# One set of angle products for both last-stage tables, sine scales from columns, and short fillers, in a fused Fourier and channel-mix kernel

## The chip, the cores and the metric

The kernel runs on one core of one Trainium2 chip. The metric is the device time of one launch in microseconds (us), the median of several runs. A core has a matrix engine (PE in the profile, with its weight loads as PEld), a vector engine (DVE), a scalar engine (ACT), a gather and iota engine that also issues the loads (POOL) and an issuing engine for stores (SP). Each works through its own instructions in the order of the program.

## The reference

```python
X = np.fft.fft(x, axis=1)          # x: 8 x 3072 x 256
X = np.fft.fft(X, axis=2)
x = X.real
x_prev = np.concatenate([zeros, x[:, :-1, :]], axis=1)
xk = mu_k * x + (1.0 - mu_k) * x_prev
xr = mu_r * x + (1.0 - mu_r) * x_prev
k = np.maximum(xk @ w_k, 0.0)      # 256 -> 1024
v = k * k @ w_v                    # 1024 -> 256
r = 1.0 / (1.0 + np.exp(-(xr @ w_r)))
out = r * v
```

## The kernel before, in words

The real part of the two-dimensional transform is built from small dense products with tables of sines that the kernel makes itself. For each of 8 batches, `fold` (L144) adds each row of x to its mirrored row on DVE, in two halves of 9 and 8 rows a partition. Stage A (`a_sum` L475 in batch 0, `a_item` L457 later) multiplies the folded rows by the table `w_pm`. Stage D (`d_units` L497) multiplies by the table `w_eo` and leaves `g_all`. The last stage (`c_item` L529) multiplies `g_all` by the table `m_cs`, which has two planes (cosine and sine, index c) of 28 slices (two for each of the NJ = 14 columns j). `halves`, `diff`, `mix_part` and `mix` then make the shifted and mixed inputs on DVE, and 48 chunks of 512 tokens go through `k_products` (L614), a ReLU on ACT (L632), a square on DVE (L639), `v_tile` (L653), `r_item` with a sigmoid (L641) and `v_out` (L664).

The last part of the program is a loop over 197 steps that is full of matmuls; the code up to L750 is the start of batch 0, written out by hand. `pin_order` (L90) fixes the order on each engine to the order in which the code is written. This is the part that the change touches.

Tables. Each table is a sine of an angle. The angles are made as outer products: rows of 128 numbers on one partition (`rw`, L267, filled by DVE with `memset` and `ts`, L255) are multiplied on PE by another such row (`outer`, L293). DVE converts the product from PSUM to whole numbers (`ts` with a factor), wraps it with a bitwise and, and ACT takes the sine.
- `w_pm`: four products with rows P0, P1, E0, E1 (L300), the conversion `u_w` (L354, L355), two sines and a scaling (L356 to L359).
- `m_cs`: `m_outer(j0, j1)` (L337) makes for both c three products (Q2, RR, PH + c; a fourth, D0 + c, for j = 0). `m_angles` and `m_wrap` (L346, L350) convert, `m_sine` (L405) takes the sine. They are called for j 0 to 4 at the start, 5 to 8 while x is loaded, 9 to 13 after stage D (L706 to L708, sine at L750).
- `w_eo`: two products (L366), conversion `ueo` (L371), sine at L432, two columns copied from PSUM (L439).
- `turn`: a permutation table, rows at L379 (called at L700), columns by PE at L388 (step 2 of the loop), `turn_table` (step 3).
- The mixing factors are turned into columns by four one-column matmuls (`mu_turn`, L205), copied at L703.

PSUM is used through two rings of slots: three of 1024 columns (`ps_w`) and two of 512 (`ps_v`). A new user of a slot waits until the last one has been read.

`keep_busy` (L182) issues fillers, matmuls of zeros with 512 columns: 8 at the very start, 7 before stage A (L687), 4 before the first `k_products` (L743).

Loads of x go out on POOL in the order of L225 to L235, with iotas for their row indices between them; the weights follow in `loads` (L415).

Of the kernel before, what the change touches and what calls it, by code (L numbers as in the profile page):

```python
# [9 lines left out]
FP32 = mybir.dt.float32  # L10
# [29 lines left out]
def kernel(  # L40
# [10 lines left out]
    nc = tc.nc  # L51
# [7 lines left out]
    NJ, NJ1, NJ2 = 14, 5, 9  # L59
# [22 lines left out]
    def ps_v():  # L82
        return ps_slot("V", 2, 512)
# [98 lines left out]
    def keep_busy(n, ps=None):  # L182

        ps = ps or ps_v()
        for _ in range(n):
            nc.tensor.matmul(out=ps[:, 0:512], lhsT=zeros, rhs=_v(zeros, 0, [(0, 4), (1, P)]),  # L186
                             start=True, stop=True)

    keep_busy(8)


    mu_row = const.tile([1, 2, 256], FP32)
    mu_p = const.tile([1, 2, 2, P], FP32)
    unit = const.tile([1, 1], FP32)
    V.memset(unit, 1.0)
    for i, mu in enumerate((moe_mu_k, moe_mu_r)):
        nc.sync.dma_start(out=mu_row[:, i], in_=mu.rearrange("(a b) -> a b", a=1))

    def mu_rows(a):
        for p0, f0, step, n in (((0, 0, 1, 1), (1, 2, 2, 63), (64, 1, 2, 64)),  # L200
                                ((0, 128, 1, 1), (1, 254, -2, 63), (64, 255, -2, 64)))[a]:
            nc.scalar.activation(out=mu_p[:, a, :, p0:p0 + n],
                                 in_=_v(mu_row, f0, [(256, 2), (step, n)]), func=AF.Copy)

    def mu_turn():  # L205
        ps = ps_w()
        for a in range(2):
            for i in range(2):
                nc.tensor.matmul(out=ps[:, 2 * a + i:2 * a + i + 1], lhsT=mu_p[:, a, i], rhs=unit,
                                 start=True, stop=True)  # L210
        return ps
# [3 lines left out]
    for xm in xm_sb:  # L215
# [8 lines left out]

    iota(ramp, pattern=[[1, P]], base=0, channel_multiplier=0)  # L225
    load_p(0, 0)
# [10 lines left out]
    m_pi = const.tile([P, 1], FP32)  # L237
    V.memset(m_pi, -math.pi)
    p_pi = const.tile([P, 1], FP32)
    V.memset(p_pi, math.pi)  # L240


# [9 lines left out]
    nc.scalar.activation(out=m_cs.rearrange("p c s t -> p (c s t)").bitcast(FP32),  # L252
                         in_=_v(zeros.bitcast(FP32), 0, [(0, 2 * NJ), (1, 64)]), func=AF.Copy)

# [7 lines left out]

    WA, WB = 4 * NU, 2 * NU
    E0, E1, P0, P1, JR, ONE, C192, Q2, RR, PH, PHS, D0, DS, Q, TR, J0, TO, SG = range(18)
    rw = const.tile([1, 18, P], FP16)  # L267
    rhs_w = const.tile([1, 4, WA + WB], FP16)
# [4 lines left out]
    def wv(n, o, *dims):  # L273
        return _v(rhs_w, (WA + WB) * n + o, list(dims))

    one = ramp[0:1]
    EVEN_ODD = [(P + 1, 2), (2, 64)]
    V.memset(rv(E0, 0, (1, 2 * P)), 0.0)
    V.memset(rv(E0, 0, *EVEN_ODD), 1.0)
    V.memset(rv(P0, 0, (1, 2 * P)), 0.0)  # L280
    V.memset(wv(0, 0, (1, 2 * (WA + WB))), 0.0)
    V.memset(wv(2, 0, (1, 2 * (WA + WB))), 48.0)
    V.memset(wv(2, 0, (4, NU)), 72.0)
    V.memset(wv(2, WA, (WA + WB + 1, 2), (2, NU)), 60.0)
    V.memset(rv(ONE, 0, (1, P)), 1.0)
    V.memset(rv(C192, 0, (1, P)), 192.0)
    ts(rv(P0, 0, *EVEN_ODD), _v(one, 0, [(1, 2), (2, 64)]), 0.0, ADD)
    for c in range(2):
        ts(wv(0, 2 * c, (WA + WB + 1, 2), (4, NU)), _v(one, 0, [(0, 2), (1, NU)]), 0.0, ADD)
        ts(wv(3, 1 + 2 * c, (4, NU)), one[:, 0:NU], -1.0, MUL, 72.0 - 24 * c, ADD)  # L290
    ts(wv(0, WA, (WA + WB + 1, 2), (2, NU)), _v(one, 0, [(0, 2), (1, NU)]), 0.0, ADD)

    def outer(out, rhs):  # L293
        for n, (row, r) in enumerate(rhs):
            nc.tensor.matmul(out=out, lhsT=rw[:, row], rhs=r, start=n == 0, stop=n == len(rhs) - 1)  # L295

    u_w = const.tile([P, WA + WB], INT32)
    w_pm = const.tile([P, 3, WA + WB], FP16)
    ps = ps_w()
    outer(ps[:, 0:WA + WB], [(row, rhs_w[:, n]) for n, row in enumerate((P0, P1, E0, E1))])  # L300

    C_0, C_1 = [(64, 2), (1, 32)], [(64, 2), (1, 32)]
    for n, v0, v1, k in ((PH, -0.25, 0.0, 47), (PHS, 0.5, -0.25, 15)):
        V.memset(rv(n, 0, *C_0), v0 * S)
        V.memset(rv(n, 32, *C_1), v1 * S)
        V.memset(rv(n, k, (64, 2)), -S / 4)

    V.memset(rv(D0, 0, (1, 2 * P)), 0.0)
    V.memset(rv(D0, 96, (P, 2), (1, 32)), S / 2)
    V.memset(rv(D0, 64 + 47, (1, 1)), 0.0)
    V.memset(rv(DS, 64 + 15, (1, 1)), S / 2)
    V.memset(rv(J0, 0, (1, NJ)), 0.0)
    V.memset(rv(J0, 0, (1, 1)), 1.0)
    ts(rv(JR, 0, (1, P)), one, 0.0, ADD)
    for g in range(2):
# [9 lines left out]
    ts(rv(Q, 64, (1, 64)), rv(Q2, 64, (1, 64)), 0.5, MUL)  # L328
    V.tensor_tensor(out=rv(PH, 64, (P, 2), (1, 64)), in0=rv(PH, 64, (P, 2), (1, 64)),
                    in1=rv(Q, 64, (0, 2), (1, 64)), op=ALU.subtract)  # L330
# [4 lines left out]
    ang_ps = {}  # L335

    def m_outer(j0, j1):  # L337
        ps = ang_ps[j0] = ps_w()
        n = j1 - j0
        for c in range(2):  # L340
            outer(ps[:, 512 * c:512 * c + 64 * n],
                  [(Q2, rv(JR, j0, (1, n), (0, 64))), (RR, rv(TR, 0, (0, n), (1, 64))),
                   (PH + c, rv(ONE, 0, (0, n), (1, 64))),
                   (D0 + c, rv(J0, 0, (1, n), (0, 64)))][:4 if j0 == 0 else 3])

    def m_angles(j0, j1):  # L346
        ts(ang[:, :, j0:j1], _v(ang_ps[j0], 0, [(512, 2), (64, j1 - j0), (1, 64)]),
           float(TURN) / S, MUL)

    def m_wrap(j0, j1):  # L350
        ts(ang[:, :, j0:j1], ang[:, :, j0:j1], TURN - 1, ALU.bitwise_and)

    m_outer(0, NJ1)
    ts(u_w, ps[:, 0:WA + WB], TURN / 96.0, MUL)  # L354
    ts(u_w, u_w, TURN - 1, ALU.bitwise_and)  # L355
    nc.scalar.activation(out=w_pm[:, 0:2], in_=_v(u_w, 0, [(0, 2), (1, WA + WB)]), func=AF.Sin,  # L356
                         bias=m_pi, scale=TWO_PI / TURN)
    nc.scalar.activation(out=w_pm[:, 2], in_=u_w, func=AF.Sin, bias=p_pi, scale=-TWO_PI / TURN)
    nc.scalar.activation(out=w_pm[:, :, WA:WA + WB], in_=w_pm[:, :, WA:WA + WB], func=AF.Copy,  # L359
                         scale=math.sqrt(0.5))  # L360
    m_angles(0, NJ1)
    m_wrap(0, NJ1)


    eo_ps = ps_w()
    outer(eo_ps[:, 0:256], [(JR, rv(JR, 0, (1, 2), (0, 2), (2, 64))),  # L366
                            (C192, rv(E0, 0, (0, 2), (1, 2), (0, 64)))])
    for e in range(2):
        outer(eo_ps[:, 256 + e:257 + e], [(E0 + e, rv(ONE, 0, (1, 1)))])
    ueo_f = ueo.rearrange("p a c b -> p (a c b)")  # L370
    ts(ueo_f, eo_ps[:, 0:256], TURN / 256.0, MUL)  # L371
    ts(ueo_f, ueo_f, TURN - 1, ALU.bitwise_and)
# [15 lines left out]
    def turn_cols():  # L388
        ps = ps_w()
        for n in range(2):  # L390
            outer(ps[:, n:n + 1], [(TO + n, rv(ONE, 0, (1, 1)))])
        V.tensor_copy(out=cols, in_=ps[:, 0:2])

    def turn_table():
        ts(turn, ramp, cols[:, 0:1], ALU.is_equal, cols[:, 1:2], MUL)
# [40 lines left out]
    def eo_rest():  # L436

        for e in range(2):
            nc.scalar.activation(out=w_eo[:, 0, 64 * e:64 * e + 1],  # L439
                                 in_=eo_ps[:, 256 + e:257 + e], func=AF.Copy)  # L440
# [245 lines left out]
    m_outer(NJ1, NJ2)  # L686
    keep_busy(7)  # L687
# [17 lines left out]
    d_half(0, 2, ps_v(), "V")  # L705
    m_outer(NJ2, NJ)  # L706
    m_angles(NJ2, NJ)
    m_wrap(NJ2, NJ)  # L708
# [34 lines left out]
    keep_busy(4, ps_w())  # L743
# [18 lines left out]
    at(2, turn_cols)  # L762
    at(3, turn_table)
# [111 lines left out]
```

## Time and profile before

| what | value |
|---|---|
| median of 3 runs | 449.67 us (447.14, 449.67, 451.22) |
| the profiled execution's own time | 450.17 us |
| its span, from the first to the last instruction | 448.4 us |
| mean granted TensorE clock | 0.983 |
| DVE busy | 361.0 us (81%) |
| ACT busy | 327.1 us (73%) |
| POOL busy | 51.6 us (12%) |
| DMA | 40.93 MB, mean 91 GB/s |

The profiled execution is 0.5 us above the median, and 1.8 us of its time lie outside its span. A line of the timeline gives start, duration, engine, source line, operation, what is written and read, shape and count; "x18" means 18 instructions merged into one line. A line of the chain gives start, duration and the work that the end of the program can be followed back to. A line of the waits gives an engine and line, what it waited for, the total, the number of times and the longest. A line of the windows gives the stretch, its length, the busy time of each engine with its count of instructions, the granted TensorE clock as a share of full speed, the DMA share and GB/s.

### The profile page before, as it was taken

To read this page: it belongs to the slowest core of one execution; us is meant where nothing else is said; L and a number is where in the kernel's file an instruction comes from. 1 tells how busy PE (TensorE), PEld (TensorE's weight loads), DVE (VectorE), ACT (ScalarE), POOL (GpSimd) and SP (SyncE) were. 2 spreads that over 40 slices of the span, in tenths; PEclk is the share of its full clock that TensorE was granted. 3 is DMA by queue.
4 is the path that set the end of the run, shared out by engine and by line. 5 is a ranking of instruction groups with operands and counts; after the bars stand their busy time and mean duration, and the time that the engine had idled before them with its cause. 6 is when DMAs were issued, how large, how long until landed. Compare 5 with 4: busy or idle time off the path is not lost.

```text
span 448.4 us, 8492 instructions
## 1 busy us (share of the span) xinstructions
PE 437.5 (98%) x3474; PEld 312.4 (70%) x3474; DVE 361.0 (81%) x530; ACT 327.1 (73%) x369; POOL 51.6 (12%) x65
## 2 busy tenths in 40 slices
PE   9889999999999999999999999999999999999995
PEld 4546777677777777777777777777777777676664
DVE  6578999999699887989789887988789755997453
ACT  6467988677777777777777877777777777666661
POOL 7751312001200040001200010000000000000000
PEclk9778999999999999999999999999999999999999
DMA  7995759236822295234932363223223232233334
GB/s 127 173 207 93 133 94 179 52 70 103 174 64 64 54 156 128 57 72 79 181 74 53 72 121 69 64 55 72 60 60 71 48 72 63 56 72 70 72 72 94
DMA packets 34507, 40.93 MB, mean 91 GB/s; under 512 B 3906, under 2 KB 30788, under 8 KB 34468
## 3 DMA queue, kind: packets, MB, share of 16 engines
q1 hardware_dynamic: 27524, 25.05, 24.4%
q0 software_dynamic: 6784, 15.21, 21.2%
q8 instruction: 27, 0.44, 0.4%
q10 hardware_dynamic: 160, 0.13, 0.1%
q14 instruction: 12, 0.10, 0.1%
HBM read 30.41 MB, written 25.17 MB: 124 GB/s over the span
## 4 chain that ended last, share of the span: by engine, by line
PE 91%; DVE 3%; ACT 2%; DMA 2%; issue 1%; POOL 0%; POOLq 0%; DVEq 0%
PE psV L660 36%; PE psW L622 36%; PE psW L646 9%; PE psW L542 3%; PE psW L504 3%; DMA xm<-in_x_dram,idx 2%; PE psW L470 2%; ACT rl L632 1%; PE psW L487 1%; DVE k L639 1%; DVE d L566 0%; DVE x L591 0%; ACT pq L450 0%; PE psW L295 0%; PE psW L186 0%
## 5 line engine op out<-in xcount | busy, mean ns | idle before, releaser
L632 ACT ACTIVATE rl<-psW 128x1024 f16<-128x1024 f32 x192 | 196.4, 1024 | 98.8 <-PE psW L622 94.1
L622 PE MATMUL psW<-x,wk 128*128 128x512 f16 (+1 forms) x776 | 198.2, 378 | 1.2 <-ACT rl L632 0.7
L660 PE MATMUL psV<-wv_sb,k 128*128 128x256 f16 x1536 | 199.1, 273 | 0.0
L660 PEld LDWEIGHTS <-k 128*128 128x128 f16 x1536 | 146.4, 98 | 27.8
L639 DVE TENSOR_TENSOR k<-rl 128x2048 f16<-128x2048 f16 (+1 forms) x98 | 117.7, 1201 | 50.9 <-ACT rl L632 46.8
L622 PEld LDWEIGHTS <-wk 128*128 128x128 f16 x776 | 76.1, 98 | 52.1 <-issue 2.6
L670 DVE SCALAR_TENSOR_TENSOR o<-psV,r 128x512 f32<-128x512 f32 (+1 forms) x97 | 66.2, 682 | 16.2 <-PE psV L660 13.7
L591 DVE TENSOR_TENSOR x<-y,t 128x1536 f16<-128x1536 f16 x60 | 57.5, 959 | 2.1
L646 PE MATMUL psW<-wr,x 128*128 128x256 f16 x384 | 49.8, 273 | 0.0
L651 ACT ACTIVATE r<-psW 128x1024 f16<-128x1024 f32 x48 | 48.9, 1018 | 0.8 <-PE psW L646 0.8
L646 PEld LDWEIGHTS <-x 128*128 128x128 f16 x384 | 37.6, 98 | 14.6 <-issue 0.3
L125 POOL DMA_INDIRECT xm<-in_x_dram,idx x25 | 31.4, 1256 | 7.9 <-issue 7.0
L122 POOL DMA_DIRECT2D xp<-in_x_dram x16 | 9.1, 568 | 199.0 <-DVE p L155 184.3
L450 ACT ACTIVATE a<-psW 128x832 f16<-128x832 f32 (+1 forms) x32 | 27.1, 848 | 3.7 <-PE psW L487 3.7
L450 ACT ACTIVATE pq<-psW 128x768 f16<-128x768 f32 (+5 forms) x32 | 27.5, 859 | 3.2 <-issue 2.5
L450 ACT ACTIVATE g_all<-psW 128x1024 f16<-128x1024 f32 (+3 forms) x39 | 28.1, 723 | 0.4 <-PE psW L504 0.4
L153 DVE TENSOR_TENSOR p<-xp,xm 96x2304 f16<-96x2304 f16 (+3 forms) x19 | 20.9, 1102 | 1.3 <-DMA xm<-in_x_dram,idx 1.3
L558 DVE TENSOR_TENSOR y<-pq 128x960 f16<-128x960 f16 (+5 forms) x38 | 18.7, 532 | 3.9 <-issue 2.1
L542 PEld LDWEIGHTS <-g_all 128*128 128x128 f16 (+1 forms) x233 | 15.3, 99 | 9.4 <-ACT g_all L450 1.1
L504 PEld LDWEIGHTS <-a 128*128 128x128 f16 x208 | 15.2, 104 | 8.2 <-ACT a L450 1.0
L578 DVE TENSOR_SCALAR t<-d,mu_m 128x1536 f16<-128x1536 f16 x32 | 19.9, 620 | 0.0
L542 PE MATMUL psW<-m_cs,g_all 128*128 128x128 f16 (+2 forms) x221 | 18.1, 222 | 0.9 <-ACT g_all L450 0.9
(101 smaller groups left out, 191.8 us busy)
## 6 DMA issues: line engine op xcount, KB each, us to landing
out_dram<-o SPq DMA_DIRECT2D x190, 128.0 KB, 2.4
xp<-in_x_dram POOLq DMA_DIRECT2D x8, 432.0 KB
xp<-in_x_dram POOLq DMA_DIRECT2D x8, 384.0 KB
wv_sb<-in_moe_w_v_dram POOLq DMA_DIRECT2D x1, 512.0 KB
xm<-in_x_dram,idx POOLq DMA_INDIRECT x25
out_dram<-o ACTq DMA_DIRECT2D x2, 64.0 KB
out_dram<-o SPq DMA_DIRECT2D x2, 64.0 KB
wk<-in_moe_w_k_dram,row_i POOLq DMA_INDIRECT x4
```

What stands on the lines that cost most here:

```text
L125: nc.gpsimd.indirect_dma_start(dst, None, src, bass.IndirectOffsetOnAxis(ap=idx, axis=0))
L450: nc.scalar.activation(out=out_ap, in_=in_ap, func=AF.Copy)
L504: nc.tensor.matmul(out=ps[:, o:o + 128], lhsT=a_t[b][:, e, 2 * (u0 + i):2 * (u0 + i) + 2, :], rhs=w_eo[:, e], start=True, stop=True)
L542: nc.tensor.matmul(out=ps[0:m, o:o + 64 * k], lhsT=g_all[:, u, 128 * min(f, 1):128 * min(f, 1) + m], rhs=m_cs[:, f % 2, sl:sl + k], start= ...
L591: V.tensor_tensor(out=dst, in0=_v(y_t[b], 64 * (NSL * a + lo + 3 * m), [(1, n)]), in1=_v(x_t["t", a], 64 * lo, [(1, n)]), op=ALU.subtract ...
L622: nc.tensor.matmul(out=st["k", ds][:, 512 * hs + lo:512 * hs + hi], lhsT=wk_sb[m][a][:, 128 * fc:128 * fc + 128], rhs=xk[:, a, 512 * i + l ...
L632: nc.scalar.activation(out=st["rl"][:, 2 * ds:2 * ds + 2], in_=st["k", ds].rearrange("p (f t) -> p f t", f=2), func=AF.Relu, bias=0.0, sca ...
L639: V.tensor_tensor(out=k2_t[c][:, lo:hi], in0=r, in1=r, op=ALU.mult)
L646: nc.tensor.matmul(out=ps[:, 256 * tb:256 * tb + 256], lhsT=x_t[b, 1, m][:, a, 512 * i + 128 * tb: 512 * i + 128 * tb + 128], rhs=wr_sb[m] ...
L651: nc.scalar.activation(out=st["r", c], in_=ps, func=AF.Sigmoid)
L660: nc.tensor.matmul(out=st["v", tb - h][:, 256 * h:256 * h + 256], lhsT=k2_t[c][:, fc, 128 * tb:128 * tb + 128], rhs=wv_sb[:, fc], start=(f ...
L670: V.scalar_tensor_tensor(out=o.rearrange("p a b -> p (a b)")[:, 0:256 * n], in0=st["v", t0][:, 0:256 * n], scalar=16.0, in1=st["r", c][:, ...
```

## The change: what it does

1. `m_cs`: `m_outer` makes one set of three products for both planes, with a row HQ in the place of the PH rows. The phases become four columns `ph_c`, made by four one-column products (PH, PH0, PHS, PHS0), and are added while DVE converts (`m_angles`: multiply, then add a column), once for each c; j = 0 has a phase of its own, so its column of 64 is converted by itself. All j are multiplied and converted at the start, in two pieces (j 0 to 5 and 6 to 13), before the first fold. The sine for j 6 to 8 follows at once; the sine for j 9 to 13 stays where it was.
2. `w_pm`: two products of 26 columns (rows PN and JR) and three short conversions; which of the even and odd columns gets a nonzero angle is decided by the scale of the sine, a column `sc` that differs between even and odd partitions. Four sines, one scaling and one negation on ACT. A new iota `pcol_i` on POOL and a bitwise and on DVE give the parity.
3. `w_eo`: one product of 128 columns, converted twice with the quarter turn as a constant; its two columns come from the parity.
4. All small products share one PSUM slot `prep`.
5. The mixing factors lie on two partitions; two matmuls in place of four, at the start.
6. `turn_rows` and the whole `turn_table`, with its two one-column products, move to between the second and the third fold of batch 0.
7. Fillers: 6 of 512 columns where 7 were, and short ones of 128 columns: 14 before the third `a_sum`, 4 after it, 6 after the fourth, 8 after the first two `d_half`, 14 (in the place of 4 long ones) before the first `k_products`.

The diff, cut to what the text speaks of:

```diff
-    NJ, NJ1, NJ2 = 14, 5, 9
+    NJ, NJ1, NJ2 = 14, 6, 9
-    keep_busy(8)
+    keep_busy(8, ps_w())
...
     iota(ramp, pattern=[[1, P]], base=0, channel_multiplier=0)
+    iota(pcol_i, pattern=[[0, 1]], base=0, channel_multiplier=1)
     load_p(0, 0)
...
+    ts(g_i, pcol_i, 1, ALU.bitwise_and)
+    for n, on, off in ((0, 0.0, TWO_PI / TURN), (1, TWO_PI / TURN, 0.0), (2, 0.0, -math.pi),
+                       (3, -math.pi, 0.0)):
+        nc.scalar.activation(out=sc[:, n:n + 1], in_=g_i, func=AF.Copy, bias=off, scale=on - off)
...
+    prep = ps_w()
+    for k, row in enumerate((PN, JR)):
+        outer(prep[:, P_W + NU * k:P_W + NU * k + NU], (row, rv(JR, 0, (1, NU))))
+    for n in range(4):
+        outer(prep[:, P_C + n:P_C + n + 1], (PH + n, rv(ONE, 0, (1, 1))))
+    def m_outer(ps, j0, j1):
+        n = j1 - j0
+        outer(ps[:, 0:64 * n], (Q2, rv(JR, j0, (1, n), (0, 64))),
+              (RR, rv(TR, 0, (0, n), (1, 64))), (HQ, rv(ONE, 0, (0, 64 * n))))
+    ang_ps = [ps_v(), ps_v()]
+    m_outer(ang_ps[0], 0, NJ1)
+    outer(prep[:, P_E:P_E + 128], (JR, rv(JR, 0, (1, 2), (2, 64))))
+    m_outer(ang_ps[1], NJ1, NJ)
+    for n, (k, ph) in enumerate(((0, 0.75), (0, 0.5), (1, 0.625))):
+        ts(u_w[:, n], prep[:, P_W + NU * k:P_W + NU * k + NU], TURN / 96.0, MUL, ph * TURN, ADD)
+    ts(u_w, u_w, TURN - 1, ALU.bitwise_and)
...
+    def m_angles(ps, j0, j1, z=0):
         for c in range(2):
+            for k0, k1, n in ((j0, j0 + z, 2 * c + 1), (j0 + z, j1, 2 * c))[1 - z:]:
+                ts(ang[:, c, k0:k1], ps[:, 64 * (k0 - j0):64 * (k1 - j0)], float(TURN) / S, MUL,
+                   ph_c[:, n:n + 1], ADD)
         ts(ang[:, :, j0:j1], ang[:, :, j0:j1], TURN - 1, ALU.bitwise_and)
+    ts(ph_c, prep[:, P_C:P_C + 4], float(TURN) / S, MUL)
+    m_angles(ang_ps[0], 0, NJ1, 1)
+    for c in range(2):
+        ts(ueo[:, :, c], _v(prep, P_E, [(64, 2), (1, 64)]), TURN / 256.0, MUL,
+           0.75 * (1 - c) * TURN, ADD)
+    ts(ueo, ueo, TURN - 1, ALU.bitwise_and)
+    m_angles(ang_ps[1], NJ1, NJ)
+    for a in range(2):
+        nc.tensor.matmul(out=prep[:, P_M + 2 * a:P_M + 2 * a + 2], lhsT=mu_p[:, a], rhs=unit,
+                         start=True, stop=True)
+    V.tensor_copy(out=mu_f.rearrange("p a i -> p (a i)"), in_=prep[:, P_M:P_M + 4])
...
     eo_rest()
-    m_outer(NJ1, NJ2)
-    keep_busy(7)
+    m_sine(NJ1, NJ2)
+    fill = ps_v()
+    keep_busy(6, fill)
     fold(0, 0, 1, 4)
     a_sum(0, 0, 0)
     fold(0, 0, 5, 4)
     a_sum(0, 0, 4)
     loads()
-    m_angles(NJ1, NJ2)
-    m_wrap(NJ1, NJ2)
-    m_sine(NJ1, NJ2)
-    mu_ps = mu_turn()
+    turn_rows()
+    turn_table()
+    keep_busy(14, fill, 128)
     fold(0, 1, 0, 4)
     a_sum(0, 1, 0)
+    keep_busy(4, fill, 128)
     fold(0, 0, 0, 1)
-    turn_rows()
     fold(0, 1, 4, 4)
     a_sum(0, 1, 4, "VA")
-    V.tensor_copy(out=mu_f.rearrange("p a i -> p (a i)"), in_=mu_ps[:, 0:4])
+    keep_busy(6, fill, 128)
     d_half(0, 0, ps_v(), "A")
     d_half(0, 2, ps_v(), "V")
-    m_outer(NJ2, NJ)
-    m_angles(NJ2, NJ)
-    m_wrap(NJ2, NJ)
+    keep_busy(8, ps_w(), 128)
     c_item(0, 0, 5, "A", True)
...
-    keep_busy(4, ps_w())
+    keep_busy(14, ps_w(), 128)
     k_products(chunks[0], 0, 0, 256)
...
-    at(2, turn_cols)
-    at(3, turn_table)
```

More of the change, by code (lines that the diff above doesn't have):

```diff
@@ L201, in mu_rows @@
                                 ((0, 128, 1, 1), (1, 254, -2, 63), (64, 255, -2, 64)))[a]:
[L202 to L211, printed above, removed]
+            nc.scalar.activation(out=mu_p[:, a, p0:p0 + n], in_=_v(mu_row, f0, [(step, n)]),
+                                 func=AF.Copy)
     for h in range(2):
@@ L270, in rv @@
+    m_pi = sc[:, 4:5]
+    for i in range(2):
+        nc.scalar.activation(out=unit[:, i:i + 1], in_=g_i[0:2], func=AF.Copy, bias=1.0 - i,
+                             scale=2.0 * i - 1.0)
+    nc.scalar.activation(out=m_cs.rearrange("p c s t -> p (c s t)").bitcast(FP32),
+                         in_=_v(zeros.bitcast(FP32), 0, [(0, 2 * NJ), (1, 64)]), func=AF.Copy)
+    JR, PN, Q2, RR, HQ, TR, PH, PH0, PHS, PHS0, TO, SG, ONE = range(13)
+    rw = const.tile([1, 13, P], FP16)
     def rv(n, o, *dims):
@@ L285 @@
[L285 to L300, printed above, removed]
     C_0, C_1 = [(64, 2), (1, 32)], [(64, 2), (1, 32)]
     for n, v0, v1, k in ((PH, -0.25, 0.0, 47), (PHS, 0.5, -0.25, 15)):
[L307 to L312, printed above, removed]
@@ L327, with outer @@
             V.memset(rv(RR, 47, (64, 2)), -S / 2)
-    ts(rv(Q, 64, (1, 64)), rv(Q2, 64, (1, 64)), 0.5, MUL)
-    V.tensor_tensor(out=rv(PH, 64, (P, 2), (1, 64)), in0=rv(PH, 64, (P, 2), (1, 64)),
-                    in1=rv(Q, 64, (0, 2), (1, 64)), op=ALU.subtract)
+    ts(rv(HQ, 64, (1, 64)), rv(Q2, 64, (1, 64)), -0.5, MUL)
+    def outer(out, *pairs):
+        for n, (row, r) in enumerate(pairs):
+            nc.tensor.matmul(out=out, lhsT=rw[:, row], rhs=r, start=n == 0,
+                             stop=n == len(pairs) - 1)
+    WA, WB = 4 * NU, 2 * NU
+    u_w = const.tile([P, 3, NU], INT32)
+    w_pm = const.tile([P, 3, WA + WB], FP16)
+    ph_c = const.tile([P, 4], FP32)
     ang = (k2_pool.tile([P, 8, 512], FP16, name="rl", tag="rl")
@@ L361 @@
[L361 to L372, printed above, removed]
+    prep = ps_w()
+    P_W, P_C, P_E, P_M, P_T = 0, 64, 128, 256, 264
```

96 lines of the change are left out of this document (36 added, 60 removed).

## The prediction

> **What bounds the kernel now.** I read the page first, then the chain of waits, then the first 46 us of it. From the page: PE is busy nearly all the time, and the row of the granted clock has its low digits in slices 2 to 4 alone (a slice is 11.2 us).
>
> ```profile
> PE 437.5 (98%) x3474; PEld 312.4 (70%) x3474; DVE 361.0 (81%) x530; ACT 327.1 (73%) x369; POOL 51.6 (12%) x65
> PEclk9778999999999999999999999999999999999999
> ```
>
> So the loop is bound by PE and is not touched by the change; what the change can give or take lies in the first 40 us, and a shift there goes to the end as it is. The chain of that stretch (start, duration, work):
>
> ```profile
> 4.50 8.52 DMA xm<-in_x_dram,idx
> ...
> 13.53 0.70 DVE p L153
> ...
> 15.70 0.59 DVE p L153
> ...
> 16.55 0.70 PE psW L487 x4
> ...
> 17.27 0.60 DVE a L448
> ...
> 17.91 1.21 PE psW L487 x6
> ...
> 19.15 0.55 ACT a L450
> ...
> 19.75 1.03 PE psV L504 x8
> 20.78 1.71 PE psW L295 x6
> 22.49 1.84 PE psW L542 x15
> 24.33 0.96 PE psW L504 x8
> 25.30 1.71 PE psW L186 x4
> 27.00 1.09 PE psW L622 x8
> ...
> 28.56 1.13 ACT pq L450 x2
> ...
> 29.71 0.82 ACT m_cs L407
> ...
> 31.38 1.82 ACT rl L632 x2
> ...
> 33.24 2.77 PE psW L622 x8
> ```
>
> The reader is to see four links: x lands (13.0), the last folds on DVE (to 16.5), a run of PE, ACT and PE (17.9 to 28.6) in which 1.71 us are angle products (L295) and 1.71 us are fillers (L186), and ACT from 28.6 to 33.2. The PE links are slow because the clock is at half there:
>
> ```profile
> 17.00:17.50 0.50, 0.08 (x1) 0.00 (x0) 0.23 (x1) 0.50 (x1) 0.19 (x2) 0.59 1.23 160
> 27.00:27.50 0.50, 0.50 (x6) 0.40 (x4) 0.46 (x2) 0.00 (x0) 0.50 (x1) 0.67 0.95 189
> 34.00:34.50 0.50, 0.50 (x3) 0.10 (x1) 0.37 (x1) 0.30 (x2) 0.00 (x0) 0.65 1.15 231
> ```
>
> The clock (last but two) falls at 17.1, rises at 27.3, falls again at 34.2. The steps lie 10.2 and 6.8 us apart, three and two times 3.41, so I read it as decided every 3.41 us. The first column says 1.00 from the start, but the stage A matmuls contradict it: they change pace in mid-run, so the clock rose near 13.7.
>
> ```profile
> L487 PE MATMUL psW<-w_pm,p x6: 381/381/381, 12.0 to 12.9; 96*128 96x208 f16 x6
> L487 PE MATMUL psW<-w_pm,p x5: 252/252/252, 13.8 to 14.2; 96*128 96x208 f16 x5
> ```
>
> **The change, step by step.** Rows for the prices (timeline: start, duration, work):
>
> ```profile
> 5.02 4.10 PE L295 MATMUL psW<-rw 1*128 1x320 f16 x18
> 5.26 0.32 DVE L257 TENSOR_SCALAR u_w<-psW 128x156 int32<-128x156 f32 x1
> ...
> 7.39 0.82 DVE L257 TENSOR_SCALAR rl<-psW 128x640 int32<-128x640 f32 x1 [1.52 <-PE psW L295]
> 8.25 0.53 DVE L257 TENSOR_SCALAR rl<-rl 128x640 int32<-128x640 int32 x1
> ...
> 9.05 3.17 PE L186 MATMUL psV<-zeros 128*128 128x512 f16 x7
> ...
> 10.27 0.69 DVE L153 TENSOR_TENSOR p<-xp,xm 96x1024 f16<-96x1024 f16 x1 [0.83 <-DMA xm<-in_x_dram,idx]
> ...
> 13.64 1.67 ACT L450 ACTIVATE a<-psW 128x832 f16<-128x832 f32 x2 [2.12 <-PE psW L487]
> ...
> 14.77 0.17 DVE L380 MEMSET rw<- 1x128 f16 x1
> ...
> 15.61 0.67 DVE L153 TENSOR_TENSOR p<-xp,xm 96x1024 f16<-96x1024 f16 x1
> ...
> 25.32 0.88 DVE L602 SCALAR_TENSOR_TENSOR x<-d,mu_f,y 128x256 f16<-128x256 f16 x2
> ...
> 33.84 0.15 DVE L392 COPY cols<-psW 128x2 f32<-128x2 f32 x1
> ...
> 34.30 1.02 ACT L632 ACTIVATE rl<-psW 128x1024 f16<-128x1024 f32 x1 [0.20 <-PE psW L622]
> ...
> 34.74 0.34 DVE L257 TENSOR_SCALAR turn<-ramp,cols 128x128 f16<-128x128 int32 x1
> ```
>
> 1. *POOL.* One small iota ahead of x's loads: no row shows one in that place; it may be free, and at most costs its own 0.2 us on every load. I take 0.1. Step 4 covers it, since the folds will wait for DVE and not for x; without that cover it is 0.1 on the end.
>
> 2. *Rows on DVE, products on PE.* DVE has some 2 us less of row making before 4.5, hidden by the first 8 fillers (8 x 0.43). PE then makes six short products (0.55), 3 x 384, 128 and 3 x 512 columns. Four fillers of 512 took 1.71, so a column is 0.83 ns at the low clock: 0.96 + 0.11 + 1.28. The 128-column product ends near 6.2, the last near 7.5. They go no deeper into the chain than the next step.
>
> 3. *Conversions on DVE.* They all sit ahead of the first fold now. From 0.32 for 156 and 0.82 for 640 columns a conversion from PSUM is 0.15 + 1.05 ns a column; a bitwise and of 640 is 0.53. When can they start? In the waits, matmuls into one half of a PSUM tile waited for the reading of the other half:
>
> ```profile
> PE psW L487 <- DVE a L448: 0.8, 1, 0.8
> PE psW L295 <- ACT rl L632: 1.4, 1, 1.4
> ```
>
> (first line). All short products share the tile `prep`, and the 128-column product is written before `u_w` reads it, so I let DVE start at 6.4, not at 4.9. Then: `u_w` 0.55, `ph_c` 0.18, j 0 to 5 with its four column-added pieces 1.5 and its and 0.5, `ueo` 0.75, j 6 to 13 1.5 and 0.6, the mixing factors 0.1: 5.6 us, so the first fold starts at 12.0 and not at 10.27. No row has a conversion with a column added; 0 to 0.13 a piece (the `turn` row, 0.34 for 128, against 0.21 by the slope of 0.53 for 640 and 0.32 for 156) bounds it; I took 0.07.
>
> 4. *Turn rows and table, moved.* The rows are 0.84 (14.77 to 15.61) and sat between folds before, so the move alone is a gain; but `turn_table` copies what PE makes after the second `a_sum`, so DVE waits for PE with the third fold queued behind it. Folds 1 and 2 (0.8 each) end at 13.7, the rows at 14.5. PE: the `mu` products wait for `ueo` (same tile), to 10.1; 6 fillers (6 x 0.43) to 12.7; sums from 13.0, four at 0.17 and twelve at 0.09 with the clock rising at 13.7 as before: 14.75, products 14.9, copy at 15.1 (0.15), table (0.34), third fold at 15.55 where it was 13.53. From there to the end of the last fold it is 2.96 less the rows, 2.1: 17.7 against 16.5. **Plus 1.2.**
>
> 5. *Angle products gone from 20.78.* From the last fold's end (16.5) to the last stage (22.5) it is 6.0 now. Of it go 1.71 of products; 8 short fillers come, 0.86 at the low clock. The short fillers bring PE to some three quarters of the step from 13.7 to 17.1, where it had about half, so I let the clock fall one step later (20.5); then the six matmuls of 17.91 take 0.6 of their 1.21. The last stage starts at 17.7 + 6.0 - 1.7 + 0.9 - 0.6 = 22.3. The old conversion on DVE (0.82 and 0.49 from 22.5) lay beside ACT and gives nothing.
>
> 6. *The 14 short fillers.* PE is busy from 20.5, so the clock is full from about 23.9. The mixed inputs were made at 26.2 (25.32 and 0.88), 3.7 after the last stage began, and the long fillers held the channel products to 27.0; at 22.3 + 3.7 = 26.0 the short ones (14 x 0.06 at full clock) are done. The products end at 26.7 (8 x 0.11, the first ahead of the second input), where the chain has 28.1, and ACT's `pq` begins at 27.3, where it has 28.56: **minus 1.25, step 4 within it.** Without the rise at 23.9 the fillers take 1.5 and the inputs still come last.
>
> 7. *A PSUM slot less in the loop.* The second waits line: the turn products waited 1.4 us for a slot, and the fourth piece of channel products behind them began at 33.24, after the second ReLU (0.9 each) and not the first. Now it takes the slot that is free first. It gains between 0.2 (ACT's idle time before the ReLU at 34.30) and 0.9; I take 0.6, since PE at the low clock is late for the pieces after it as well.
>
> 8. *ACT.* Five more small instructions before 5.1, two more sines, and the sine for j 6 to 8 ahead of the sums, done by 13.3; the first sum comes at 14.1 (13.64 after 2.12 idle now). Hidden; without that idle time it would cost some 0.9.
>
> Sum: -1.25 - 0.6 = -1.85 on the profiled execution's 450.17: 448.3. The median stands 0.5 below that execution, so I say **447.8**.
>
> **The rivals.**
>
> *A. The clock never falls after 13.7.* For it: the fillers leave no idle time on PE of more than a microsecond. Against it: no longer one stood before the fall at 17.1 (0.83 us). Then stage D, its fillers and the last stage take half: last stage at 21.3, inputs 3.3 later at 24.6, products' end at 25.4 where I have 26.7, slot 0.6: minus 3.1, 446.6. [...]
>
> *B. DVE is not late.* If the conversions start at 4.9, or the copy finds its product made, the last fold ends at 16.3 and the sum is 1.4 better: 446.4. With A as well: 445.1. For it: DVE idles 1.5 us before 7.39 now. Against: the shared tile.
>
> *C. Slower: the clock does not rise at 13.7.* PE now stands idle from 7.5 to 9.6 and the fillers end at 12.7, so the step from 10.3 to 13.7 is 91% busy, where it was full. The 8 fillers from 1.0 (about 70% of a step) did not raise it. If 91% is too little, the 16 sums take 1.0 more, and DVE waits for them with the third fold; the 8 and 14 fillers and the last stage at the low clock then cost 1.8 beside my case. Together -1.85 + 1.0 + 1.8 = +0.95: 451.1, and 450.6 by the median. It decides where the last fold ends after 19.6: there the later gain (1.2 + 1.85) is eaten.
>
> *D. It does not do what it says:* the fillers do not change the clock at all and only stand in the way. Then the 0.6 of step 5 and some 0.7 of step 6 are lost: 449.1.
>
> **How the numbers follow.** The measurement cannot tell less than about 1% (4.5 us) from no change. My case 0.42 (447.8); A alone 0.14 (446.6); B alone 0.10 (446.4); A with B 0.13 (445.1, over the bound of 445.2); D 0.05 (449.1); C 0.12 (450.6); something worse than that, by over 1%, 0.04. Faster by over 1%: A with B and a tail of A, 0.14; slower by over 1%: 0.05 with a tail of C; within 1%: 0.81. The range leaves out about half of A with B, half of C and what is worse: 444.8 to 450.9.
>
> **What would show it.** Right: the first fold near 12.0 and the third near 15.5, with DVE waiting for PE ahead of the copy of `cols`; the last fold near 17.7; no L295 at 20 us; the last stage near 22.3; `pq` of the second part near 27.3; the fourth channel piece not behind a slot. Wrong: a first fold at 10.3 (B), sums of 0.17 to the end of stage A (C), a clock column of 1.00 from 17 to 27 (A). A change of the loop after 45 us would also make me wrong; I see none.

## The result, and the profile after

The changed kernel took 445.89 us in the median of 12 runs (445.39 to 447.61), the kernel before 449.58 (447.14 to 451.22) beside it. By the medians that is 3.7 us less. The ratio is 0.9934, with a 95% interval from 0.9912 to 0.9955, which means 2.0 to 4.0 us. The lowest runs lie 1.8 us apart and the highest 3.6. The profiled execution took 445.67 us, 443.87 of them its span, where the one before took 450.17 with a span of 448.40.

The page of the changed kernel, first the PE row, then the granted clock in 40 slices:

```profile
PE 430.4 (97%) x3496; PEld 309.5 (70%) x3496; DVE 359.8 (81%) x520; ACT 328.1 (74%) x378; POOL 51.9 (12%) x66
...
PEclk8899999999999999999999999999999999999999
```

PE is busy 7.1 us less although it has 22 instructions more, and the low digits of slices 3 and 4 (22 to 45 us) are gone. The same three windows as before the change, with the clock in the last column but two:

```profile
17.00:17.50 0.50, 0.42 (x7) 0.25 (x6) 0.30 (x2) 0.38 (x1) 0.45 (x1) 1.00 1.11 150
27.00:27.50 0.50, 0.50 (x6) 0.34 (x4) 0.48 (x2) 0.49 (x1) 0.50 (x2) 1.00 1.10 221
34.00:34.50 0.50, 0.43 (x4) 0.14 (x3) 0.50 (x2) 0.49 (x3) 0.00 (x0) 1.00 1.06 208
```

All three stood at 0.59 to 0.67. In this execution the clock's record begins at 4.0 us; it is full to 7.4, at half to 14.25, and full from there to the end: neither the fall at 17.1 nor the one at 34.2 happens. The chain of the first 33 us of the changed kernel (start, duration, work):

```profile
5.20 0.38 DVE u_w L240 x3
...
8.44 0.98 PE psW L358 x4
9.42 2.67 PE psV L185 x6
12.10 2.54 PE psW L472 x16
14.63 0.14 PE psW L300 x2
...
15.26 0.69 DVE p L153
...
16.53 0.61 DVE p L153
...
17.39 0.54 PE psW L472 x4
...
18.60 0.71 PE psW L472 x6
...
19.34 0.55 ACT a L435
...
19.93 0.62 PE psV L489 x8
20.55 0.45 PE psW L185 x8
...
21.02 0.70 PE psW L527 x9
...
24.47 0.92 PE psW L607 x7
...
25.86 1.13 ACT pq L435 x2
...
27.01 0.82 ACT m_cs L392
...
28.68 3.64 ACT rl L617 x4
```

Read it against the chain before. The last fold ends 0.85 us later (17.35, where it was 16.5), but the last stage starts at 21.02 and not at 22.49, and the first ReLU is followed at 28.68, 2.7 us earlier than 31.38. The links that became short are PE's: eight stage D matmuls take 0.62 where they took 1.03, eight short fillers 0.45 where six angle products took 1.71. Between 29 and 41 us another 1.8 us are won (the end comes 4.5 us earlier), beside the second fall of the clock that is missing.

### The profile page after: what moved, and what is told of

The parts are those of the page before. It is cut to its first block, busy times and chain, and to the rows that moved or that the text cites. A ratio compares the mean times of both kernels' runs of the same rounds, so it can differ in the third digit from the quotient of the medians.

```text
span 443.9 us, 8536 instructions
## 1 busy us (share of the span) xinstructions
PE 430.4 (97%) x3496; PEld 309.5 (70%) x3496; DVE 359.8 (81%) x520; ACT 328.1 (74%) x378; POOL 51.9 (12%) x66
## 4 chain that ended last, share of the span: by engine, by line
PE 89%; DVE 7%; ACT 3%; issue 1%
PE psV L645 36%; PE psW L607 35%; PE psW L631 9%; PE psW L527 2%; PE psW L489 2%; PE psW L455 2%; ACT rl L617 1%; DVE k L624 1%; DVE x L587 1%; DVE p L153 1%; PE psW L185 1%; PE psW L472 1%; DVE d L551 1%; PE psV L185 1%; ACT pq L435 1%
## 5 line engine op out<-in xcount | busy, mean ns | idle before, releaser
L655 DVE SCALAR_TENSOR_TENSOR o<-psV,r 128x512 f32<-128x512 f32 (+1 forms) x97 | 66.1, 682 | 16.2 <-PE psV L645 13.7
L435 ACT ACTIVATE pq<-psW 128x768 f16<-128x768 f32 (+5 forms) x32 | 27.4, 859 | 1.3 <-PE psW L527 1.3
L489 PEld LDWEIGHTS <-a 128*128 128x128 f16 x208 | 14.1, 98 | 7.7 <-issue 0.6
```

Source lines behind the costliest of these rows:

```text
L435: nc.scalar.activation(out=out_ap, in_=in_ap, func=AF.Copy)
L655: V.scalar_tensor_tensor(out=o.rearrange("p a b -> p (a b)")[:, 0:256 * n], in0=st["v", t0][:, 0:256 * n], scalar=16.0, in1=st["r", c][:, ...
```

## The experiments

Two theories stood against each other. The clock theory: PE's clock changes in steps of 3.41 us (between its changes lie 3.41, 6.83 and 10.24 us in the trace of the kernel before), how much full-height work PE was given in one step sets the clock of the next, the short fillers keep it at full speed, and that is the gain. The work theory: the gain is the work that left the path (late angle products, their conversions, a PSUM slot). A third question was what the moved turn table gives away. The share of a step, below, is the full-height work that PE was given in it (columns x rows / 128) as a part of what it could take at full clock; the last section works it out. Each kernel ran 12 times, the one with the turn table back in the loop 9 times. Times in the first group stand beside 449.96 us for the kernel before on the same chip, in the second beside 449.35, in the third beside 449.81, and in the last beside 448.66.

### The short fillers taken away

```diff
-    keep_busy(14, fill, 128)
...
-    keep_busy(4, fill, 128)
...
-    keep_busy(6, fill, 128)
...
-    keep_busy(8, ps_w(), 128)
...
-    keep_busy(14, ps_w(), 128)
+    keep_busy(4, ps_w())
```

> The changed kernel without its 32 short fillers ahead of the last stage, and with the 4 long ones ahead of the first channel products as before. If the short fillers are what keeps the clock up (theory), the granted clock falls within 7 us of the end of stage A, the matmuls of stage D and the last stage take 0.107 us and not 0.056, the clock may fall again behind the last stage, and the time is 448 to 449 us. If the clock held for another reason, the missing idle time at 20 us or the phase of the clock's steps (rival), the time stays at 445.5 to 446.3 and the clock at full.

Measured: 448.83 us (447.07 to 452.15), ratio 0.9978, interval 0.9954 to 1.0001. The clock rises at 13.7, falls at 17.2 and stays at half until 27.4, as it did before the change. The timeline of PE in this kernel (in brackets the idle time ahead of the group):

```profile
16.45 0.93 PE L472 MATMUL psW<-w_pm,p 96*128 96x208 f16 x8 [1.44 <-DVE p L155]
...
19.20 1.20 PE L472 MATMUL psW<-w_pm,p 96*128 96x208 f16 x6 [0.68 <-DVE a L433]
```

The same six sums take 1.20 us here and 0.71 in the changed kernel. Without the fillers the rest of the change is worth 1.1 us by the medians (0 to 2.1 by the interval), of the 2.2 to 3.7 that the whole change was worth in three measurements. And in the step ahead of the fall no idle time of PE is longer than 1.44 us.

### The short fillers one row high

```diff
-            nc.tensor.matmul(out=ps[:, 0:cols], lhsT=zeros,
...
+            r = P if cols == 512 else 1
+            nc.tensor.matmul(out=ps[:, 0:cols], lhsT=zeros[0:r],
...
```

> The changed kernel with its 46 short fillers made one row high (one partition of zeros times one partition of zeros, the same 128 columns): the same PE time in the records. If PE's recorded busy time decides the clock, the time stays at 445.5 to 446.3. If the rows in use count (the stretch of one-row products before 9 us did not raise the clock in the kernel before), the clock falls as without the fillers, and the time is that of the kernel without them, 448 to 449.

Measured: 451.61 us (450.23 to 452.37), ratio 1.0032, interval 1.0016 to 1.0049. The windows of this kernel, cut at the steps of its clock:

```profile
13.60:17.00 3.40, 2.77 (x36) 2.42 (x35) 2.37 (x11) 1.62 (x2) 2.70 (x3) 1.00 1.07 146
17.00:20.40 3.40, 2.22 (x15) 1.39 (x14) 1.06 (x3) 0.86 (x1) 2.57 (x4) 0.50 1.25 196
```

and the windows of the changed kernel at a step of its own clock and the one behind it:

```profile
17.70:21.10 3.40, 2.40 (x33) 1.90 (x31) 1.10 (x2) 1.43 (x3) 2.77 (x4) 1.00 1.30 210
21.10:24.50 3.40, 2.77 (x39) 2.01 (x40) 2.13 (x7) 2.11 (x3) 1.62 (x2) 1.00 1.13 203
```

With one-row fillers PE is busy for 2.77 us of the step from 13.6, and the clock falls behind it and stays at half until 34.1. In the changed kernel 2.40 us were enough to keep it. So busy time alone does not tell the two apart: the same columns with one row of the array in use did not hold the clock. The time lies above both expected ranges, and 2.8 us above the kernel without short fillers on the same chip. A part of that is likely not the cost of one-row work: that kernel has four long full-height fillers ahead of the first products, where this one has one-row fillers alone, and its clock rose again at 27.4 and not at 34.1.

### The turn table made behind the fourth fold

```diff
     turn_rows()
-    turn_table()
     keep_busy(14, fill, 128)
...
     fold(0, 1, 4, 4)
+    turn_table()
     a_sum(0, 1, 4, "VA")
```

Its two products also go into the fillers' PSUM slot here, and not into `prep`.

> The turn table (its two products, the copy and the table) moved behind the fourth fold; the rows stay. The third fold then waits for the rows and the load alone (13.5 in place of 15.26). If the wait of DVE for PE ahead of the copy sits on the chain, the last fold ends 1.7 us earlier, at 15.6, and the time falls by 1.3 to 1.7 us, to some 444.4. Rival: the sums on PE (to 14.5) and the scalar engine's copies take its place, and it gains under 0.5.

Measured: 451.00 us (448.64 to 453.31), ratio 1.0024, interval 0.9999 to 1.0050. The third fold did start early (13.62), but the time got worse. Part of it is in this kernel's chain:

```profile
17.05 0.13 PE psV L300 x2
17.18 0.98 PE psW L472 x4
...
18.19 0.17 DVE cols L379
...
18.38 0.56 DVE turn L240
...
19.28 0.71 PE psW L472 x6
```

The two products now stand behind the sums of the third and fourth fold on PE, so DVE waits 2.5 us for them and the copy that the last six sums need waits behind it on DVE. Moving the wait moved what is queued behind it. It does not explain all of the 5 us that this kernel lies above the changed one; see the last runs.

### The last sine made early, behind the second sum

```diff
     a_sum(0, 0, 4)
+    m_sine(NJ2, NJ)
     loads()
...
-    m_sine(NJ2, NJ)
```

> The sine for the last five columns (1.65 us on the scalar engine, 27.0 to 28.7 in the changed kernel) moved behind the second sum's copy, where the engine idles from 15.5 to 17.1. If that engine bounds the stretch from 25.9 to 32.2, the time falls by 1.0 to 1.6 us, to some 444.6. Rival: the vector engine, which the chain shows from 32.3, keeps the end where it is: under 0.5.

Measured: 449.40 us (445.59 to 450.96), ratio 0.9975, interval 0.9947 to 1.0002. No gain over the changed kernel, and its runs spread over 5 us. The first ReLU does start 0.7 us after the copy of the last channel piece (2.2 in the changed kernel), but that piece comes 4 us late. Half of it is a clock that rose only at 19.3 in this execution: in the next run of the changed kernel, with a rise at 19.4, the piece is 1.9 us late. For the other half, the chain of this kernel:

```profile
24.45 1.41 PE psW L489 x8
...
25.88 1.19 ACT pq L435 x2
```

The eight matmuls L489 take 0.62 us in the changed kernel, at the same granted clock; here what waits for them goes on 0.8 us later, and ACT's first copy is released at that moment and not when its own matmuls were done, 2.1 us before.

### The changed kernel again, and the kernel before with the short fillers alone

> The changed kernel as it is, once more, so that the other kernels of this batch have it on their own chip. Both theories expect what it took before: 445.9 us, between 445.0 and 447.5, and every run within 2.5 us of the others, because the short fillers hold PE's clock at full speed from about 14 us on in most executions.

Measured: 445.83 us (445.25 to 447.67), ratio 0.9927, interval 0.9903 to 0.9950.

```diff
+    keep_busy(14, fill, 128)
     mu_ps = mu_turn()
...
+    keep_busy(4, fill, 128)
...
+    keep_busy(6, fill, 128)
...
-    keep_busy(4, ps_w())
+    keep_busy(14, ps_w(), 128)
```

> The kernel before with the changed kernel's short fillers alone: 14, 4 and 6 of 128 columns at the three places between the folds, 14 of 128 columns in place of the 4 long ones ahead of the first products; the tables, the turn table's place and the late angle products stay as they were. Theory 1 (the gain is the clock: PE's clock is decided anew every 3.41 us by how many full-height columns PE was fed, and the fillers keep it at full speed through the last stage): most of the gain comes without the rest of the change, 446.0 to 447.5 us, and the granted clock does not fall at 17 us. Theory 2 (the gain is the work taken off the path, the late angle products, their conversion and the PSUM slots): 449 to 450 us.

Measured: 446.98 us (445.10 to 449.30), ratio 0.9957, interval 0.9925 to 0.9989. By the medians these fillers alone bring 2.4 of the 3.5 us, and the rest of the change 1.1 more, as much as it brought without them. The intervals leave 0.5 to 3.4 us for the fillers and 0 to 2.1 for the rest, so the split is not sharp. Up to the first ReLU (line `rl`) the profiles give all of it to the fillers. The ReLUs in this kernel, and behind them those of the changed kernel:

```profile
28.54 2.81 ACT L632 ACTIVATE rl<-psW 128x1024 f16<-128x1024 f32 x3
32.36 1.02 ACT L632 ACTIVATE rl<-psW 128x1024 f16<-128x1024 f32 x1 [1.01 <-PE psW L622]
...
28.58 4.63 ACT L617 ACTIVATE rl<-psW 128x1024 f16<-128x1024 f32 x5
```

The first stands at 28.54 and 28.58, the fourth at 32.36 and 31.30. What the rest of the change brings comes behind the third ReLU. The windows of the kernel with the fillers alone, at the steps of its clock:

```profile
13.50:16.90 3.40, 3.40 (x42) 3.28 (x41) 2.55 (x12) 3.06 (x4) 2.49 (x4) 1.00 0.95 133
16.90:20.30 3.40, 2.42 (x31) 1.94 (x29) 0.79 (x3) 1.76 (x3) 2.79 (x4) 1.00 1.29 194
...
27.20:30.60 3.40, 1.24 (x8) 0.60 (x7) 3.33 (x7) 3.39 (x5) 2.79 (x3) 1.00 1.12 204
30.60:34.00 3.40, 3.40 (x10) 1.24 (x9) 2.17 (x5) 1.78 (x2) 0.10 (x1) 0.50 1.13 207
```

No fall at 17 us any more. One at 30.6 stays, after a step in which PE waits behind the turn products for a slot and issues 8 matmuls. Four of the 12 runs had a mean clock near 0.978 and took 448.9 to 449.3; four had 0.999 and took 445.1 to 445.6, as the five fastest of the changed kernel beside them did (445.3 to 445.6). So where these fillers hold the clock, they alone seem to be worth the whole change. That it is the phase of the clock's steps that decides where they do is argued from the mean clocks, as one execution alone was profiled.

### The late angle products put back

```diff
-    m_outer(ang_ps[1], NJ1, NJ)
+    m_outer(ang_ps[1], NJ1, NJ2)
...
-    m_angles(ang_ps[1], NJ1, NJ)
+    m_angles(ang_ps[1], NJ1, NJ2)
...
-    keep_busy(8, ps_w(), 128)
+    late = ps_w()
+    m_outer(late, NJ2, NJ)
+    m_angles(late, NJ2, NJ)
```

> The changed kernel with angle columns 9 to 13 multiplied and converted behind the last fold again, in place of the 8 short fillers there; one set of products and all other fillers stay. Theory 1 (clock): the products are one row high and carry no weight for the clock, as the run with one-row fillers showed, so that the step around 18 to 21 us sinks from 0.46 to 0.33 of PE's full-height columns and the clock falls: 448 to 449 us and a half clock somewhere from 20 to 30 us. Theory 2 (work on the path): 0.5 us of products and about 1.1 us of conversions come back ahead of the last stage, without any fall: 446.9 to 447.6 us.

Measured: 446.15 us (445.57 to 448.21), ratio 0.9945, interval 0.9919 to 0.9970. Both theories missed. With one set of products and a full clock, products and conversions behind stage D cost 0.3 us by the medians, less than the runs can tell apart; taking them off the path was not the bulk of the gain. And the clock did not fall, although the eight full-height fillers were gone: a share of 0.33 held it here, where 0.34 did not without the fillers.

### The turn table back in the loop

```diff
     turn_rows()
-    turn_table()
...
+    at(2, turn_cols)
+    at(3, turn_table)
```

> The changed kernel with the turn table's two products, its copy and the table itself made in steps 2 and 3 of the loop again, as before the change; the rows for it stay early. The third fold then starts when the one ahead of it is done, about 13.9 us where it was 15.26. Theory 1 (the move costs 1.2 us at the third fold and saves 0.6 us in the loop, as forecast): 445.3 us, 0.6 us less than the changed kernel on the same chip. Rival (the third fold is not what the last stage waits for, or what it gains is lost again because PE stands idle and its clock falls): 445.7 to 448 us.

Measured: 445.40 us (444.52 to 446.26), ratio 0.9912, interval 0.9883 to 0.9942, 0.43 less than the changed kernel on the same chip with overlapping ranges. It is the lowest median of all, near what theory 1 had, though not surely better than the changed kernel. In the profiled execution (446.26 us, the highest of the nine) the third fold starts at 14.04, the first ReLU at 27.47, 1.1 us before the changed kernel's, but the fifth at 32.24, later than the changed kernel's 32.20. Two views of this kernel say why, the waits:

```profile
PE psW L300 <- ACT rl L620: 1.4, 1, 1.4
```

and the windows:

```profile
27.00:30.40 3.40, 1.24 (x8) 0.73 (x8) 3.22 (x7) 3.28 (x4) 2.61 (x4) 1.00 1.11 204
30.40:33.80 3.40, 3.40 (x19) 2.16 (x18) 3.12 (x6) 2.58 (x3) 0.00 (x0) 0.50 1.16 216
```

The turn products wait 1.4 us for a slot, PE issues 8 matmuls in that step, the clock falls for the next one, and the 1.1 us are gone. Whether the faster executions (from 444.52 on) had this fall is not known, as they have no profile.

### Split turn table, and the last sine moved to the front

The products stay early, copy and table go behind the last fold:

```diff
     turn_rows()
-    turn_table()
+    turn_products()
...
     fold(0, 1, 4, 4)
+    turn_table()
```

> The changed kernel with the turn table's step cut in two: rows and the two products stay where the change put them, the copy and the table (0.16 and 0.35 us of VectorE) go behind the last fold, where VectorE is idle for 0.6 us, so that no fold waits for a product on PE and no PSUM slot is taken in the loop. Theory 1 (the third fold's delay of 1.2 us is what the change gives away, and what the run with the table in the loop gained early it lost again to the slot): third fold at 14.0 us, and 0.9 to 1.3 us less than the changed kernel, 444.6 to 445.0 us, ratio to before 0.990. Rival (the delay is covered, as the last stage waits for something else): third fold as early, time as the changed kernel's, 445.6 to 446.2 us.

The sine for j 6 to 13 in one, ahead of the sums:

```diff
-    m_sine(NJ1, NJ2)
+    m_sine(NJ1, NJ)
...
-    m_sine(NJ2, NJ)
```

> The changed kernel with the sine of angle columns 9 to 13 made right behind that of columns 6 to 8, where ScalarE is idle, and no longer between the last channel piece and the first relu. Theory 1 (the two sines of 0.83 us stand on ScalarE ahead of the first relu and nothing else does): the first relu comes 1.2 to 1.6 us earlier and the end 0.6 to 1.2 us, since VectorE's mixes of 3 us stand behind the same pieces: 444.7 to 445.3 us. Rival (VectorE sets the pace from 27 us on, and the first copy of sums on ScalarE starts 0.5 us later): 445.6 to 446.4 us.

> Both edits of the two runs before it. If their gains lie on one chain one behind the other, they add: 443.7 to 444.5 us. If a faster stage leaves PE idle for long enough that its clock falls between 27 and 34 us, as in the run with the table in the loop, 444.8 to 446 us, and the granted clock shows the fall.

Measured: the split 449.56 us (445.86 to 452.30), ratio 0.9997, interval 0.9965 to 1.0029; the sine 449.22 (446.05 to 450.27), ratio 0.9995, interval 0.9969 to 1.0021; both 448.39 (446.25 to 450.41), ratio 0.9966, interval 0.9939 to 0.9993. All three lie 2.4 to 3.4 us above the highest time that either theory had. The third fold did come early (13.63 in the first, 14.06 in the third). The timeline of the first of them:

```profile
26.59 1.12 PE L529 MATMUL psV<-m_cs,g_all 128*128 128x128 f16 x12
...
29.41 1.34 ACT L437 ACTIVATE pq<-psV 128x512 f16<-128x512 f32 x2 [4.19 <-PE psW L609]
```

The copies read what these twelve matmuls make. The first copy needs the first six, which are done at 27.18 by the records, and starts at 29.41, 2.2 us later, at a granted clock of 1.00. In the changed kernel the same copy starts 0.04 us after its first six matmuls. The step in which ACT, DVE and in the end PE waited was nearly empty (a share of 0.13), and the clock fell behind it (32.2 to 39.0). The profile of the sine alone shows much less of this: its execution took 446.05 us, the fastest of the 12, its copies of the channel pieces follow their matmuls by 0.04 us, and the first copy of sums is 0.7 us late.

> The changed kernel as it is, a third time. In five runs (the late turn table, both early sines, the split turn table, and the last two together) copies on ScalarE started 1 to 2 us after the matmuls that they wait for had ended by the records, at a full granted clock; none of the profiles of the changed kernel shows that, but neither of those five had the changed kernel beside it. If it is those kernels' order that brings the delay, the changed kernel takes 445.4 to 446.3 us once more, its copies follow their matmuls within 0.1 us. If it comes with the place where a kernel runs, it can come here too: 448 to 450 us, with the first copy of channel sums 0.8 us late or more.

Measured: 446.43 us (445.52 to 447.69), ratio 0.9944, interval 0.9920 to 0.9969, 0.1 above the range expected, and the copies of the channel pieces 0.04 us after their matmuls. So the changed kernel took 445.8 to 446.4 us in each of its three measurements. That does not settle what holds PE up in the five kernels, since the changed kernel was never run beside them, in the first and the third group.

The traces hold one more sign, the times of PE's semaphore updates, by which it tells the other engines that matmuls are done. In the three profiles of the changed kernel, and in the three other kernels of the second group, each update comes 0.01 us after the recorded end of its matmul. In all seven profiles of the first and the third group some updates come 0.2 us late or more and some are missing from the trace, also with the short fillers taken away or made one row high; the profile of the kernel before shows the same. So the place, or the hour, takes part. The order of the work seems to take part too: without the fillers or with one-row ones no copy of sums or channel pieces is more than 0.3 us late, in the five kernels the latest of each is 0.7 to 3.7 us late. What delays PE there is not settled, as the matmuls' starts are recorded, their ends are modelled, and no recorded wait covers the time. What the five edits cost by themselves stays open.

## Why the prediction was right in the number and wrong in one step

447.8 was forecast, 445.89 came, inside the range and within 1% of before. The likeliest case was not what happened, and the gain came out at 3.7 us where 1.9 were forecast. That the time lies inside the range is owed to the width of the range, not to the case that I put first.

1. *POOL.* Covered, as said: the first fold starts at 10.80, behind DVE's copy at 10.73 and not behind x.

2. and 3. *Products and conversions.* The products took half the time forecast (the last ended at 5.81, not 7.5), since in this execution the clock was full from 4.0 to 7.4; in the repeated run, with a clock that rose only at 19.4, they ended at 7.2. So DVE began at 5.20 and not at 6.4, right behind the 128-column product, as forecast. In the two later profiles of the changed kernel, with the clock's rise at 13.7 and 19.4, it began at 5.97 and 5.96 and the first fold at 11.6, near the 12.0 forecast. From DVE's start to the first fold it took 5.60 us where the sum said 5.6; the column-added pieces and the first fold are in the timeline of the changed kernel:

```profile
5.91 1.39 DVE L240 TENSOR_SCALAR rl<-psV,ph_c 128x64 int32<-128x64 f32 x4
...
8.70 1.39 DVE L240 TENSOR_SCALAR rl<-psV,ph_c 128x512 int32<-128x512 f32 x2
...
10.80 0.68 DVE L153 TENSOR_TENSOR p<-xp,xm 96x1024 f16<-96x1024 f16 x1
...
14.80 0.16 DVE L379 COPY cols<-psW 128x2 f32<-128x2 f32 x1 [1.26 <-PE psW L300]
```

Two times 1.39 stand against two times 1.5. The start is near the 4.9 of rival B, but by luck: the early full clock brought it, not B's reason, as DVE did wait for the shared tile.

4. *Turn table.* Right in kind: DVE waits 1.26 us for PE ahead of the copy, and the third fold starts at 15.26 (15.55 forecast). The last fold is 0.85 late, not 1.2. At the end of the program the move does not even cost that: with the table back in the loop the median was 0.43 lower.

5. *The failed step: "so I let the clock fall one step later (20.5)".* It did not fall at all, so rival A came about, at a chance of 0.14, and along its path: the last stage began at 21.02 (21.3 in A) and the first channel products ended at 25.39 (25.4). I judged a step by PE's busy share (the step that fell had "about half", the new one "three quarters") and did not work out the next steps. By full-height work the steps from 14.25 stand at 0.53, 0.46, 0.59 and 0.88 of what the array can take; the one before the old fall at 0.34. What I held against A was also misread: the 0.83 us of idle time lie behind the fall at 17.1, and the longest in the step ahead of it is 0.34. Nor was it a long gap of PE that brought the falls near 17 us: in the steps ahead of them PE had no gap above 0.34 us in the kernel before and none above 1.44 us without the fillers.

6. *Channel products.* `pq` began at 25.86, not at 27.3, nearly all of it step 5: the last stage began 1.3 earlier than forecast, and the inputs followed in 3.0 us and not 3.7.

7. *The slot.* The first four ReLUs now run back to back (28.58, 29.49, 30.39, 31.30), where the fourth was 0.3 late before and the fifth 0.9 more: from the first to the fifth it is 3.62 us where it was 4.82. The 1.2 us between them, which hold a part of the slow clock from 34.2 on, are twice the 0.6 of the sum and lie above the bound of 0.9. What I missed is what came to the clock behind the wait: the step with the 1.4 us of waiting had a share of 0.31, and the clock was at half from 34.2 to 37.6. This second fall went as well, and it goes with the turn products in the loop and not with the fillers. It came with the fillers alone (at 30.6) and with the table back in the loop (at 30.4, where it cost a lead of 1.1 us), and it did not come without the fillers, where the table is early. Three of the five kernels with late copies also had a fall (at 25.5, 32.2 and 34.1) without the products in the loop, behind the delays of PE that stay unexplained. The first ReLU is 2.7 us early and the end 4.5.

8. *ACT.* Hidden, as said: the first sum is copied at 13.52 after 1.17 us of idle time.

The sum by experiments, by medians with the intervals named above: fillers (clock) 2.4 us, everything else together 1.1, of it 0.3 the angle products, which the runs cannot tell from nothing. By the profiles most of the 1.1 is the slot and the second fall, so the clock again in part.

## What to carry to other kernels

Where PE waits for others in a start-up stage, price the clock first: cut the windows at its steps (3.41 us here) and add up columns times rows, not busy time alone. Short full-height fillers in PE's idle time were worth about twice what all the other edits were, by the medians, and one-row work that looks as busy did not hold the clock (2.77 us of a step, where 2.40 us with full-height fillers held it). And measure a reordering beside the kernel that it changes: five kernels with one or two links freed ended 2.5 to 5 us above the changed kernel, but it was not run beside them, and how much of that is theirs is not known.

## What the runs showed of the hardware

*The share of a step, and the clock in the next.* The trace of the kernel before has its clock changes at 13.67, 17.09, 27.33, 34.15 and 37.57 us, that of the changed kernel at 4.01, 7.43 and 14.25: one, two or three times 3.41 us apart. From the fourteen profiles I took 165 such steps, from the step ahead of the first recorded rise up to 46 us, and added, for each matmul, columns x 0.417 ns x rows / 128. (The unit is half of the 0.833 ns a column at which the 512-column fillers ahead of the first rise follow each other, 427 ns apart in the median of both kernels; the loop's 512-column matmuls follow each other 215 to 216 ns apart, 0.42 ns a column.) In these 165 steps a share of 0.39 or more was followed by a full clock in all 125 cases, 0.31 or less by half in all 21; between, in 19 cases, both came. Of the steps at full clock, those of 0.36 or more were never followed by a fall, and those of 0.345 or less always, but for the one of 0.33 with the late products. These are counts for the first 46 us of these kernels; no run looked for a limit. For instance the PE groups of the changed kernel in its step from 14.25:

```profile
L472 PE MATMUL psW<-w_pm,p 96*128 96x208 f16 x15 | 2.0, 266 | 0.6 <-DVE p L155 0.6
L185 PE MATMUL psV<-zeros 128*128 128x128 f16 x18 | 1.3, 220 | 0.0
```

13 of the 15 sums start in it: 13 x 208 x 0.75 + 18 x 128 = 4332 columns, 1.81 us, 0.53 of the step. A step at half clock that full-height work fills stands at 0.50 (in the kernel before the one from 23.9, ahead of the rise at 27.3). In that kernel's step from 3.4 two long fillers and one-row products kept PE busy throughout, the share was 0.13, and the first rise came at 13.67. In the second profile of the changed kernel the steps from 9.2 and 12.6 stand at 0.38 and 0.34, and the rise came at 19.4.

*The steps began at another time in other executions.* The first rise was recorded at 3.9 to 5.0, at 13.4 to 13.7 and at 19.3 to 19.4 us, in the same kernel too (4.0, 13.7 and 19.4 in three executions of the changed one). The stretch ahead of the first recorded rise counts as full in the mean clock of a run. Much of the spread goes with that mean: of 32 runs of the kernel before, the eight with a mean clock of 0.972 or 0.973 took 450.5 to 451.5 us, the eight with 0.990 or more 446.8 to 447.4. That the phase is behind it is likely but not shown, since these runs have no profile.
